# Linear attention with soft mixture of experts on one core: first weight, v, phi and row sums moved

## The chip, the core and the metric

The kernel runs on one core of a Trainium2 chip. The time is device microseconds of that core, the median of three runs. A profile is one execution taken by the hardware profiler; its span is a little shorter than the run's time, since it counts from the first instruction to the last.

The engines are named as in the profile: PE is TensorE (matrix products, with PEld for its weight loads), DVE is VectorE, ACT is ScalarE, POOL is GpSimd, SP only issues transfers. Transfers run on 16 DMA engines, fed by queues: q1 takes those issued by SP and ACT, q0 those issued by POOL, q8 brings instructions.

## The reference

Two steps follow each other. First a linear attention with decay over 768 time steps for 4 batches and 8 heads of size 48; then a layer of soft mixture of experts over the 3072 resulting rows of 384 numbers, with 8 experts of 4 slots.

```python
# attention, for each batch and head: state is D x D
for t in range(S):
    cur = outer(u * k[t], v[t])
    y[t] = r[t] @ (state + cur)
    state = w[:, None] * state + outer(k[t], v[t])

# mixture: x is (N, Dm) = (3072, 384), phi is (Dm, 32)
logits = x @ phi
d = exp(logits) / sum over rows          # dispatch
slot_input = d.T @ x                     # 32 x 384, 4 rows for each of 8 experts
slot_out[e] = relu(slot_input[e] @ w1[e]) @ w2[e]    # w1[e]: 384 x 1024, w2[e]: 1024 x 384
c = exp(logits) / sum over slots         # combine; its sums are the "row sums"
out = c @ slot_out                       # 3072 x 384, f32
```

All inputs and the output are f32. r, k, v are 4.72 MB each, w1 and w2 12.58 MB each, the output 4.72 MB.

## The kernel before

The attention is computed in chunks of 128 time steps, three chunks and two heads at a time: 32 such steps, the loop over i. For each pair of heads m, k and r are scaled by powers of w (`scale`, by POOL from m = 1 on) into `kr`, turned by PE (`t_pe`), and v is cast to bf16 (`v_cast`, by ACT) and put in order by PE with the selection matrix `Q3`. Batches live in three buffers `raw[0..2]`; batch 3 uses `raw[0]` again once batch 0 is used up, and the second-layer weights later take `raw[1]` and `raw[2]`.

The expert weights are loaded by POOL, which casts them to bf16 on the way: first the eight w1, then the eight w2, the last w2 in three parts. `W_AT` says how many are issued in which step. All r, k, v are issued by SP. A small copy into `guard`, which reads one column of the last r, keeps POOL from issuing the first weight before that r has landed.

Routing (logits, their exponentials, the dispatch sums) is done in the loop as rows become complete. After the loop come the first expert layer, the second (`second`, for four experts at a time), the row sums with their reciprocals, and the output: 24 tiles of 128 rows, whose products with `so` are scaled by DVE and ACT in turn and stored in nine transfers. `busy(n)` issues n matmuls whose result is not used, which keep PE's clock up.

```python
    warm = LexpT[:, 2048:2560]
    late = LexpT[:, 2560:3072].bitcast(f32)
    ident_f = late[:, 0:128]
    phi_f = late[:, 128:128 + nM * ES].rearrange("p (m s) -> p m s", m=nM)
    # ... cut ...
    wu = cst.tile([8, 128], f32, name="wu")
    wu3 = wu[:].rearrange("q (e s) -> q e s", s=64)
    O(dve.memset(wu[:], 1.0))
    O(sp.dma_start(out=w_row, in_=w.rearrange("(o h) d -> o (h d)", o=1)))
    O(act.preload_act_table_set("natural_log_exp_and_others"))
    O(dve.memset(warm, 0.0))
    O(dve.memset(one_f, 1.0))
    zt = cst.tile([128, nQ, 3, P2], f32, name="zt")
    O(dve.memset(zt[:], 0.0))
    # ... cut ...
    def load_kr(which, src, b, h0, h1):
        O(sp.dma_start(out=raw_of(which, b).rearrange("p (h x) -> p h x", h=H)[:, h0:h1, :],
                       in_=src[b, h0:h1].rearrange("h (p j) d -> p h (j d)", j=J)))

    def load_v(b, h0, h1):
        O(sp.dma_start(out=raw_of(2, b).rearrange("p (h x) -> p h x", h=H * G)[:, h0 * G:h1 * G, :],
                       in_=v[b, h0:h1].rearrange("h (g p j) d -> p (h g) (j d)", g=G, j=JV)))

    def load_batch(b, step):
        for h0 in range(0, H, step):
            load_kr(0, k, b, h0, h0 + step)
            load_kr(1, r, b, h0, h0 + step)
            load_v(b, h0, h0 + step)

    load_batch(0, 2)
    load_batch(1, 2)
    O(sp.dma_start(out=phi_f, in_=moe_phi.rearrange("(mo p) s -> p mo s", p=128)))
    load_batch(2, H)

    def load_w(n, y0=0, y1=nF):
        if n < E:
            O(pool.dma_start(out=w1_all[:, n, :, :],
                             in_=moe_w1[n].rearrange("(p mo) f -> p mo f", p=128)))
        else:
            O(pool.dma_start(out=w2_of(n - E)[:, y0:y1, :],
                             in_=moe_w2[n - E].rearrange("(p y) d -> p y d", p=128)[:, y0:y1, :]))

    def keep_warm(n, bank=Yb, data=None):
        data = warm if data is None else data
        for _ in range(n):
            O(pe.matmul(bank[:, 0:512], data[:, 0:128], data[:, 0:512], start=True, stop=True))

    # ... cut ...
    QW = 2 * C + JV - 1 + C
    Q3 = cst.tile([128, QW], bf, name="Q3")
    O(pool.memset(Q3[:], 0.0))
    O(pool.affine_select(out=Q3[:], in_=Q3[:], compare_op=ALU.not_equal, fill=1.0, base=JV - 1,
                         pattern=[[-1, QW]], channel_multiplier=JV))
    O(pool.dma_start(out=wu3[0:4, :, 0:D], in_=w.rearrange("(q e) d -> q e d", e=2)))
    O(pool.dma_start(out=wu3[4:8, :, 0:D], in_=u.rearrange("(q e) d -> q e d", e=2)))
    mask_ut = cst.tile([128, 128], f32, name="mask_ut")
    O(pool.memset(mask_ut[:], 0.0))
    O(pool.affine_select(out=mask_ut[:], in_=mask_ut[:], compare_op=ALU.is_ge, fill=1.0, base=0,
                         pattern=[[-1, 128]], channel_multiplier=1))
    # ... cut ...
    def scale(m, j):
        b, q = divmod(m, nQ)
        kr = kr_t[m % NKR]
        src = raw_of(j, b).rearrange("p (h j d) -> p j h d", h=H, j=J)[:, :, 2 * q:2 * q + 2, :]
        eng = dve if m == 0 else pool
        O(eng.tensor_mul(kr[:, j].rearrange("p j (h s) -> p j h s", s=64)[:, :, :, 0:D], src,
                          W[j][:, q].rearrange("p j (h d) -> p j h d", h=2)))
    # ... cut ...
    pend = []
    W_AT = {14: 2, 15: 1, 16: 1, 18: 1, 19: 1, 20: 1, 22: 1, 23: 1, 25: 1, 26: 5}
    T_AT = {-4: [(tt, 0, 1), (tt, 1, 1), (ex, 0, 1), (tt, 0, 2)], -3: [(ex, 1, 1), (ex, 0, 2)],
            -1: [(tt, 1, 2), (ex, 1, 2)], 0: [(tt, 0, 3), (ex, 0, 3)], 1: [(tt, 1, 3), (ex, 1, 3)]}
    Z_AT = {-3: 0, -1: 1, 1: 2, 2: 3}
    # ... cut ...
            let_ev(n0 - 1, None, dve)
        if 0 <= i < nH:
            y_pe(i)
            y_evac(i)
        if odd and 0 <= mu + 3 < nU:
            scale(mu + 3, 0)
        if not odd and 0 <= mu + 2 < nU:
            scale(mu + 2, 1)
        route(i, 0)
        if 0 <= mu + 2 < nU:
            t_pe(mu + 2, odd)
            route(i, 1)
            t_evac(mu + 2, odd)
            if odd and i < 0:
                b_pe(mu + 2)
                b_evac(mu + 2)
        else:
            route(i, 1)
        if odd == 0 and 0 <= mu + 2 < nU:
            v_cast(mu + 2)
        route(i, 2)
    # ... cut ...
        if i == 2:
            O(pool.memset(ones[:], 1.0))
            for t in Le_t:
                O(pool.memset(t[:], 0.0))
        if i == 3:
            load_batch(B - 1, H)
        if 3 <= i < 3 + nM:
            O(act.copy(phi_s[:, i - 3, :].rearrange("p (j g s) -> p g j s", g=2, s=Spe),
                       phi_f[:, i - 3, :].rearrange("p (g j s) -> p g j s", g=2, s=Spe)))
        if i == 28:
            O(pool.memset(uns, 0.0))
        if i == min(W_AT):
            O(pool.tensor_copy(guard[:], raw_of(1, B - 1)[:, 0:1]))
        for _ in range(W_AT.get(i, 0)):
            load_w(nw)
            nw += 1
    assert nw == 2 * E - 1
    for y0, y1 in ((0, 4), (4, 6), (6, 8)):
        load_w(nw, y0, y1)
    # ... cut ...
    def busy(n):
        keep_warm(n, Ab[:, 1, :], w1_all[:, 0, 0, :])
    # ... cut ...
    rsr = cst.tile([128, nN], f32, name="rsr")

    def row_sums(a, z):
        for i in range(a, z):
            O(pe.matmul(Mb[:, i:i + 1], LexpT[:, i:Nn:nN], ones[:, 0:1],
                        start=(i == a), stop=(i == z - 1), skip_group_check=True))

    def row_recip(a, z):
        O(dve.reciprocal(rsr[:, a:z], Mb[:, a:z]))
    # ... cut ...
    def second(g, experts):
        for y in range(nF):
            for x in range(2):
                for j in experts:
                    O(pe.matmul(SO[x][32 * j:32 * j + 32, :], hT[g][:, y, 32 * j:32 * j + 32],
                                w2_of(g * EG + j)[:, y, x * HD:(x + 1) * HD],
                                start=(g == 0 and y == 0), stop=(g == 1 and y == nF - 1), skip_group_check=True))

    second(0, range(EG))
    busy(1)
    second(1, range(EG - 2))
    row_sums(8, nN)
    row_recip(8, nN)
    busy(3)
    second(1, (EG - 2,))
    busy(1)
    second(1, (EG - 1,))
    so = cst.tile([128, Dm], bf, name="so")
    O(dve.tensor_scalar_mul(so[:, 0:HD], SO[0], csr[:, 0:1]))
    O(act.activation(out=so[:, HD:Dm], in_=SO[1], func=AF.Copy, scale=csr[:, 0:1]))
    # ... cut ...
    out_v = out.rearrange("(p n) m -> p n m", n=nN)
    ob = [T1[:].bitcast(f32), T0[:].bitcast(f32), Ab0, Vb[:], Xb[:], Yb[:]]
    sizes = [1, 1, 2, 2, 2, 4, 4, 4, 4]
    obuf = ([raw[0][:, 16 * Dm:17 * Dm], raw[0][:, 17 * Dm:18 * Dm], Wf[0][:, 0:2 * Dm], Wf[1][:, 0:2 * Dm],
             Wf[0][:, 2 * Dm:4 * Dm]]
            + [raw[0][:, x * 4 * Dm:(x + 1) * 4 * Dm] for x in range(4)])

    def emit(i, bank, dst, x0, x1, eng):
        op = ob[bank % 6][:, 0:x1 - x0]
        O(pe.matmul(op, LexpT[:, i:Nn:nN], so[:, x0:x1], start=True, stop=True))
        if eng is dve:
            O(dve.tensor_scalar_mul(dst[:, x0:x1], op, rsr[:, i:i + 1]))
        else:
            O(act.activation(out=dst[:, x0:x1], in_=op, func=AF.Copy, scale=rsr[:, i:i + 1]))

    i = 0
    for gi, sz in enumerate(sizes):
        o_s = obuf[gi][:, 0:sz * Dm].rearrange("p (n m) -> p n m", m=Dm)
        i0 = i
        for j in range(sz):
            if i < 2:
                emit(i, 2 * i, o_s[:, j, :], 0, HD, dve)
                emit(i, 2 * i + 1, o_s[:, j, :], HD, Dm, act)
            else:
                emit(i, i + 2, o_s[:, j, :], 0, Dm, (dve, act)[i % 2])
            i += 1
        O((sp, pool)[gi % 2 if gi > 1 else 0].dma_start(out=out_v[:, i0:i, :], in_=o_s))
```

Of the kernel before, what the change touches and what calls it, by code (L numbers as in the profile page):

```python
# [9 lines left out]
def kernel(  # L10
# [13 lines left out]
    B, H, S, D = r.shape  # L24
    C = 128
    nC = S // C
    Nn, Dm = out.shape
    ES = moe_phi.shape[1]
    E = moe_w1.shape[0]
    F = moe_w1.shape[2]  # L30
    Spe = ES // E
    nM = Dm // C
# [6 lines left out]
    nN = Nn // C  # L39
# [4 lines left out]
    JV = T // C  # L44

    f32 = mybir.dt.float32
    bf = mybir.dt.bfloat16
# [4 lines left out]
    def O(ins):  # L52
        return tc.keep_in_program_order(ins)

    pe, dve, act, pool, sp = nc.tensor, nc.vector, nc.scalar, nc.gpsimd, nc.sync

    big = ctx.enter_context(tc.tile_pool(name="big", bufs=1))
    cst = ctx.enter_context(tc.tile_pool(name="cst", bufs=1))
# [6 lines left out]
    EG = E // 2  # L65
# [8 lines left out]
    def raw_of(which, b):  # L74
        return raw[b % NR][:, which * RW:(which + 1) * RW]
# [6 lines left out]
    Xb = psb.tile([128, 512], f32, name="Xb")  # L82
# [15 lines left out]
    warm = LexpT[:, 2048:2560]  # L98
    late = LexpT[:, 2560:3072].bitcast(f32)
    ident_f = late[:, 0:128]  # L100
    phi_f = late[:, 128:128 + nM * ES].rearrange("p (m s) -> p m s", m=nM)
    wu = cst.tile([8, 128], f32, name="wu")
    wu3 = wu[:].rearrange("q (e s) -> q e s", s=64)
    O(dve.memset(wu[:], 1.0))
    O(sp.dma_start(out=w_row, in_=w.rearrange("(o h) d -> o (h d)", o=1)))
    O(act.preload_act_table_set("natural_log_exp_and_others"))
    O(dve.memset(warm, 0.0))
    O(dve.memset(one_f, 1.0))
    zt = cst.tile([128, nQ, 3, P2], f32, name="zt")
# [2 lines left out]
# [13 lines that stand above are left out]

    load_batch(0, 2)
    load_batch(1, 2)
    O(sp.dma_start(out=phi_f, in_=moe_phi.rearrange("(mo p) s -> p mo s", p=128)))
    load_batch(2, H)

    def load_w(n, y0=0, y1=nF):
# [7 lines left out]
# [3 lines that stand above are left out]
# [9 lines left out]
    Q3 = cst.tile([128, QW], bf, name="Q3")  # L151
    O(pool.memset(Q3[:], 0.0))
    O(pool.affine_select(out=Q3[:], in_=Q3[:], compare_op=ALU.not_equal, fill=1.0, base=JV - 1,
                         pattern=[[-1, QW]], channel_multiplier=JV))
    O(pool.dma_start(out=wu3[0:4, :, 0:D], in_=w.rearrange("(q e) d -> q e d", e=2)))
    O(pool.dma_start(out=wu3[4:8, :, 0:D], in_=u.rearrange("(q e) d -> q e d", e=2)))
    mask_ut = cst.tile([128, 128], f32, name="mask_ut")
    O(pool.memset(mask_ut[:], 0.0))
    O(pool.affine_select(out=mask_ut[:], in_=mask_ut[:], compare_op=ALU.is_ge, fill=1.0, base=0,
# [53 lines left out]
    ones = cst.tile([128, 128], bf, name="ones")  # L213
    Le_t = [cst.tile([128, L, 128], bf, name=f"Le{j}") for j in range(2)]
    phi_s = cst.tile([128, nM, ES], bf, name="phi_s")
    acc = cst.tile([128, NA], f32, name="acc")
    guard = cst.tile([128, 1], f32, name="guard")
    st = {}
# [71 lines left out]
    def a_pe(i):  # L290
        m, b, q, g, n = at(i)
        kT, rT = st["kT", m], st["rT", m]
        for c in range(L):
            t = slice((g * L + c) * C, (g * L + c + 1) * C)
            for e in range(2):
                s = slice(64 * e, 64 * e + 64)
                O(pe.matmul(Ab[:, e, c * C:(c + 1) * C], kT[s, t], rT[s, t]))  # L297
# [129 lines left out]
    def disp_ev(n, ds_p):  # L427
        if n == 0:
            O(dve.tensor_copy(acc[:], ds_p))
        else:  # L430
            O(dve.tensor_add(acc[:], acc[:], ds_p))
# [28 lines left out]
            xt_ev(*ch[s])  # L460

    pend = []
    W_AT = {14: 2, 15: 1, 16: 1, 18: 1, 19: 1, 20: 1, 22: 1, 23: 1, 25: 1, 26: 5}
    T_AT = {-4: [(tt, 0, 1), (tt, 1, 1), (ex, 0, 1), (tt, 0, 2)], -3: [(ex, 1, 1), (ex, 0, 2)],
            -1: [(tt, 1, 2), (ex, 1, 2)], 0: [(tt, 0, 3), (ex, 0, 3)], 1: [(tt, 1, 3), (ex, 1, 3)]}
    Z_AT = {-3: 0, -1: 1, 1: 2, 2: 3}
# [25 lines left out]
    for i in range(-5, nH):  # L492
        mu, odd = divmod(i, 2)
        if 0 <= i + 1 < nH:
            a_pe(i + 1)
            mask_f(i + 1)
        if pend:
            disp_ev(*pend.pop())
        if i == nH - 1:
            turn(n0, (2,), Vb[:].bitcast(bf), act)  # L500
            disp(n0 - 1, ds_t)
            le_t(n0 - 1)
# [4 lines that stand above are left out]
        if 0 <= i + 2 < nH:  # L507
            v_pe(i + 2)
            v_evac(i + 2)
        if 0 <= i + 1 < nH:  # L510
            m_pe(i + 1)
            z_evac(i + 1)
        if odd == 0 and 0 <= mu + 1 < nU:
            prod_f(mu + 1)
        if odd and i > 0 and mu + 2 < nU:
# [19 lines that stand above are left out]
        if i == nH - 3:  # L535
            turn(n0, (0, 1), T0, act)
        if i == nH - 2:
            turn(n1, (0, 1), T1, act)
        for f, j, q in T_AT.get(i, ()):
            f(j, q)  # L540
        if i in (-4, -3):
            wu_steps(i + 4)
        if i in Z_AT:
            q = Z_AT[i]
            O(act.activation(out=zt[:, q, 2, :], in_=zt[:, q, 0, :], func=AF.Copy, scale=wT[:, q:q + 1]))
        if i == 2:
            O(pool.memset(ones[:], 1.0))
            for t in Le_t:
                O(pool.memset(t[:], 0.0))
        if i == 3:  # L550
            load_batch(B - 1, H)
        if 3 <= i < 3 + nM:
            O(act.copy(phi_s[:, i - 3, :].rearrange("p (j g s) -> p g j s", g=2, s=Spe),
                       phi_f[:, i - 3, :].rearrange("p (g j s) -> p g j s", g=2, s=Spe)))
        if i == 28:
            O(pool.memset(uns, 0.0))
        if i == min(W_AT):
            O(pool.tensor_copy(guard[:], raw_of(1, B - 1)[:, 0:1]))
        for _ in range(W_AT.get(i, 0)):
            load_w(nw)  # L560
            nw += 1
# [9 lines left out]
    def busy(n):  # L571
        keep_warm(n, Ab[:, 1, :], w1_all[:, 0, 0, :])
# [33 lines left out]
    for g in range(2):  # L606
        for a in range(2):
            for mi in range(nM):
                for j in range(EG):
                    O(pe.matmul(hb[g][a][32 * j:32 * j + 32, 0:FH], uns[:, mi, g, j, :],  # L610
                                w1_all[:, g * EG + j, mi, a * FH:(a + 1) * FH],
                                start=(mi == 0), stop=(mi == nM - 1), skip_group_check=True))
# [9 lines left out]
# [7 lines that stand above are left out]
# [14 lines left out]
# [6 lines that stand above are left out]
                                start=(g == 0 and y == 0), stop=(g == 1 and y == nF - 1), skip_group_check=True))  # L649

    second(0, range(EG))
    busy(1)
    second(1, range(EG - 2))
    row_sums(8, nN)
    row_recip(8, nN)
    busy(3)
    second(1, (EG - 2,))
    busy(1)
    second(1, (EG - 1,))
    so = cst.tile([128, Dm], bf, name="so")  # L660
    O(dve.tensor_scalar_mul(so[:, 0:HD], SO[0], csr[:, 0:1]))
    O(act.activation(out=so[:, HD:Dm], in_=SO[1], func=AF.Copy, scale=csr[:, 0:1]))

    out_v = out.rearrange("(p n) m -> p n m", n=nN)
    ob = [T1[:].bitcast(f32), T0[:].bitcast(f32), Ab0, Vb[:], Xb[:], Yb[:]]
# [13 lines left out]
# [8 lines that stand above are left out]
            else:  # L687
                emit(i, i + 2, o_s[:, j, :], 0, Dm, (dve, act)[i % 2])
            i += 1
        O((sp, pool)[gi % 2 if gi > 1 else 0].dma_start(out=out_v[:, i0:i, :], in_=o_s))  # L690


# [28 lines left out]
```

The softmax here doesn't subtract the row's maximum and nothing guards it: scores larger than these inputs give would overflow.

## Time and profile before

| what | value |
|---|---|
| median of three runs | 123.75 us (123.72 to 124.0) |
| span of the profile | 122.5 us |
| PE busy | 104.6 us, 85% |
| DVE busy | 96.1 us, 78% |
| ACT busy | 83.5 us, 68% |
| POOL busy | 60.2 us, 49% |
| HBM read, written | 39.38 MB, 4.72 MB |
| scaling by POOL (`kr<-raw,W`) | 30 times, mean 1422 ns |
| row sums on PE (`Mb<-ones,LexpT`) | 24 times, between 95.7 and 101.1 us |
| phi's transfer | one, 48 KB, 5.4 us to landing |
| loads of w and u for `wu` by POOL | one each, 1.5 KB, 4.1 and 4.5 us to landing |
| weight transfers of 768 KB, w1 and w2 | median 13.6 and 19.2 us from issue to landing |

Several engines are busy for most of the span, but their sums do not tell which of them sets the end. A busy share is an average over stages; to find the bound one asks at the end of the span what was waited for last, and follows that back. The sizes of the weight transfers are those in SBUF, as bf16; twice as much is read. The time from issue to landing of a weight is mostly time in the queue behind earlier weights.

### The profile page before, as it was taken

To read this page: it belongs to the slowest core of one execution; us is meant where nothing else is said; L and a number is where in the kernel's file an instruction comes from. 1 tells how busy PE (TensorE), PEld (TensorE's weight loads), DVE (VectorE), ACT (ScalarE), POOL (GpSimd) and SP (SyncE) were. 2 spreads that over 40 slices of the span, in tenths; PEclk is the share of its full clock that TensorE was granted. 3 is DMA by queue.
4 is the path that set the end of the run, shared out by engine and by line. 5 is a ranking of instruction groups with operands and counts; after the bars stand their busy time and mean duration, and the time that the engine had idled before them with its cause. 6 is when DMAs were issued, how large, how long until landed. Compare 5 with 4: busy or idle time off the path is not lost.

```text
span 122.5 us, 4314 instructions
## 1 busy us (share of the span) xinstructions
PE 104.6 (85%) x1790; PEld 83.2 (68%) x1792; DVE 96.1 (78%) x185; ACT 83.5 (68%) x184; POOL 60.2 (49%) x72
## 2 busy tenths in 40 slices
PE   5996797799999999999999999999979997796000
PEld 1465586687788988898888888888855885663000
DVE  6799999999999999899999899999834500299000
ACT  4459668798969998888898888898844500299000
POOL 7729534599999998895877591101000000012000
PEclk9999779999999999999999999999999999999955
DMA  2999999999999999999999999999999998069992
GB/s 57 301 367 367 375 371 370 312 389 364 308 376 382 314 161 210 209 223 214 211 218 217 212 215 215 213 221 211 220 215 212 217 207 159 10 243 381 403 415 98
DMA packets 21173, 31.79 MB, mean 260 GB/s; under 512 B 1377, under 2 KB 18274, under 8 KB 21154
## 3 DMA queue, kind: packets, MB, share of 16 engines
q0 software_dynamic: 3024, 14.55, 54.8%
q1 hardware_dynamic: 18130, 16.96, 41.1%
q8 instruction: 14, 0.23, 0.7%
q14 instruction: 5, 0.04, 0.1%
HBM read 39.38 MB, written 4.72 MB: 360 GB/s over the span
## 4 chain that ended last, share of the span: by engine, by line
PE 43%; DMA 18%; DVE 18%; ACT 7%; issue 4%; POOL 1%; POOLq 0%; DVEq 0%; ACTq 0%
DMA raw<-in_moe_w_dram 18%; PE T L233 7%; PE Vb L282 6%; PE Ab L297 4%; PE Yb L350 4%; DVE prod L255 4%; PE T L245 3%; PE Yb L142 3%; DVE AT L302 3%; PE Mb L323 3%; DVE raw L675 2%; PE Xb L385 2%; PE Yb L363 2%; PE Xb L378 2%; ACT rT L239 2%
## 5 line engine op out<-in xcount | busy, mean ns | idle before, releaser
L226 POOL TENSOR_TENSOR kr<-raw,W 128x576 bf16<-128x576 f32 x30 | 42.2, 1422 | 13.7 <-PE T L233 5.4
L302 DVE TENSOR_TENSOR AT<-Ab,mask_ut 128x768 bf16<-128x768 f32 x32 | 30.3, 946 | 0.8 <-PE Ab L297 0.6
L282 PE MATMUL Vb<-v_bf,Q 128*128 128x96 bf16 x288 | 18.2, 211 | 0.0
L233 PE MATMUL T<-ident,kr 128*128 128x128 bf16 x192 | 16.9, 227 | 1.0 <-POOL kr L226 1.0
L282 PEld LDWEIGHTS <-Q 128*128 128x128 bf16 x288 | 16.4, 101 | 1.5
L239 ACT COPY kT<-T 128x768 bf16<-128x768 bf16 x16 | 12.8, 801 | 4.5 <-PE T L233 3.3
L239 ACT COPY rT<-T 128x768 bf16<-128x768 bf16 x16 | 12.8, 801 | 4.5 <-PE T L233 3.8
L255 DVE TENSOR_TENSOR prod<-T,kT 128x768 bf16<-128x768 bf16 x16 | 15.2, 948 | 0.0
L340 DVE TENSOR_TENSOR dv<-vn,Mb 128x288 bf16<-128x288 bf16 x32 | 14.1, 441 | 0.0
L233 PEld LDWEIGHTS <-kr 128*128 128x128 bf16 x192 | 12.5, 101 | 1.8 <-POOL kr L226 1.2
L288 ACT CAST vn<-Vb 128x288 bf16<-128x288 f32 x32 | 13.4, 419 | 0.1
L339 DVE TENSOR_TENSOR Z<-Mb,zt 128x288 bf16<-128x288 f32 (+1 forms) x32 | 12.7, 397 | 0.8
L370 ACT CAST x<-Yb 128x288 bf16<-128x288 f32 x32 | 13.1, 410 | 0.2
L690 POOL DMA_DIRECT2D out_dram<-W x1 | 0.5, 549 | 25.5 <-DVE W L675 25.5
L297 PE MATMUL Ab<-rT,kT 64*128 64x128 bf16 x192 | 11.1, 222 | 1.5 <-DVE AT L302 1.4
L323 PE MATMUL Mb<-vn,kn 128*128 128x96 bf16 (+2 forms) x80 | 11.3, 239 | 0.0
L350 PE MATMUL Yb<-vn,AT 128*128 128x48 bf16 x192 | 10.4, 186 | 0.1
L268 ACT CAST v_bf<-raw 128x576 bf16<-128x576 f32 x15 | 10.2, 678 | 0.0
L136 POOL DMA_DIRECT2D raw<-in_moe_w_dram x10 | 5.5, 552 | 8.7 <-ACT Le L400 3.5
L363 PE MATMUL Yb<-dv,ident 128*128 128x288 bf16 x32 | 9.3, 289 | 0.2
L350 PEld LDWEIGHTS <-AT 128*128 128x128 bf16 x192 | 7.1, 97 | 3.4 <-issue 0.2
L297 PEld LDWEIGHTS <-kT 64*128 64x128 bf16 x192 | 5.6, 95 | 5.1 <-DVE AT L302 1.4
(142 smaller groups left out, 223.2 us busy)
## 6 DMA issues: line engine op xcount, KB each, us to landing
w_all<-in_moe_w_dram POOLq DMA_DIRECT2D x8, 768.0 KB, 13.6
raw<-in_moe_w_dram POOLq DMA_DIRECT2D x7, 768.0 KB, 19.2
raw<-in_k_dram SPq DMA_DIRECT2D x8, 288.0 KB, 6.2
raw<-in_r_dram SPq DMA_DIRECT2D x8, 288.0 KB, 6.0
raw<-in_v_dram SPq DMA_DIRECT2D x8, 288.0 KB, 6.1
raw<-in_k_dram SPq DMA_DIRECT2D x2, 1152.0 KB, 10.5
raw<-in_r_dram SPq DMA_DIRECT2D x2, 1152.0 KB, 10.1
raw<-in_v_dram SPq DMA_DIRECT2D x2, 1152.0 KB, 11.3
```

What stands on the lines that cost most here:

```text
L226: O(eng.tensor_mul(kr[:, j].rearrange("p j (h s) -> p j h s", s=64)[:, :, :, 0:D], src, W[j][:, q].rearrange("p j (h d) -> p j h d", h=2)))
L233: O(pe.transpose(bank[:, x * C:(x + 1) * C], kr[:, j, x, :], ident[:]))
L239: O(act.copy(t[:].rearrange("p (s j) -> p s j", j=J), bank[:, 0:S].rearrange("p (j s) -> p s j", j=J)))
L255: O(dve.tensor_mul(pr[:].rearrange("p (s j) -> p s j", j=J), T1[:, 0:S].rearrange("p (j s) -> p s j", j=J), st["kT", m][:].rearrange("p (s ...
L282: O(pe.matmul(Vb[:, c * P2:(c + 1) * P2], Q3[:, o:o + C], vb[:, :, g, j, :], start=(j == 0), stop=(j == JV - 1)))
L288: O(act.copy(vn[:].rearrange("p c e d -> p (c e d)"), Vb[:, 0:L * P2]))
L297: O(pe.matmul(Ab[:, e, c * C:(c + 1) * C], kT[s, t], rT[s, t]))
L302: O(dve.tensor_mul(AT[:], Ab[:, :, 0:T].rearrange("p e (c t) -> p e c t", c=L), mask_ut[:, None, None, :].to_broadcast([128, 2, L, C])))
L323: O(pe.matmul(o, kn[:, g * L + c, :], vc, start=first, stop=True, skip_group_check=True))
L340: O(dve.tensor_mul(dv[:], st["v", i][:].rearrange("p c e d -> p (c e) d"), Mb[:, 288:288 + 2 * L, None].to_broadcast([128, L * 2, D])))
L350: O(pe.matmul(Yb[:, o:o + D], AT[:, e, c, :], vn[:, c, e, :], start=first, stop=False, skip_group_check=True))
L370: O(act.copy(st["x", n][:, :, q * P2:(q + 1) * P2], Yb[:, 0:L * P2].rearrange("p (c e) -> p c e", c=L)))
```

## The change

The change has five parts.

- The first weight is issued one step of the loop sooner (step 13, one weight in steps 13 and 14 each in place of two in step 14), and the guard before it reads the last k in place of the last r.
- The last batch's v is loaded in four transfers of two heads each in place of one.
- phi is loaded with three neighbouring rows to a partition, so that each partition gets one piece of 384 B in place of three of 128 B. Then row 3p + j is where row 128 m + p is wanted. PE puts it in order with the selection matrix `Q3`, which did the same for v: nine small matmuls into `Xb`, between a cast by ACT before and a copy by ACT after.
- The two small loads of w and u into `wu` are issued by ACT at the beginning in place of POOL.
- The row sums of tiles 8 to 23 and their reciprocals, and most filler matmuls, are taken out of the wait for the last weights. Tiles 8 to 11 follow the second layer; tiles 12 to 17 and 18 to 23 are done within the output part, when six and twelve tiles have been issued.

What it is for: the weights' transfers begin sooner, small packets are fewer, and PE has nothing else in its order when the last weights land.

```diff
--- before.py
+++ after.py
@@ -98,12 +98,14 @@
     warm = LexpT[:, 2048:2560]
     late = LexpT[:, 2560:3072].bitcast(f32)
     ident_f = late[:, 0:128]
-    phi_f = late[:, 128:128 + nM * ES].rearrange("p (m s) -> p m s", m=nM)
+    phi_f = late[:, 128:128 + nM * ES]
     wu = cst.tile([8, 128], f32, name="wu")
     wu3 = wu[:].rearrange("q (e s) -> q e s", s=64)
     O(dve.memset(wu[:], 1.0))
     O(sp.dma_start(out=w_row, in_=w.rearrange("(o h) d -> o (h d)", o=1)))
     O(act.preload_act_table_set("natural_log_exp_and_others"))
+    O(act.dma_start(out=wu3[0:4, :, 0:D], in_=w.rearrange("(q e) d -> q e d", e=2)))
+    O(act.dma_start(out=wu3[4:8, :, 0:D], in_=u.rearrange("(q e) d -> q e d", e=2)))
     O(dve.memset(warm, 0.0))
     O(dve.memset(one_f, 1.0))
     zt = cst.tile([128, nQ, 3, P2], f32, name="zt")
@@ -125,7 +127,7 @@
 
     load_batch(0, 2)
     load_batch(1, 2)
-    O(sp.dma_start(out=phi_f, in_=moe_phi.rearrange("(mo p) s -> p mo s", p=128)))
+    O(sp.dma_start(out=phi_f, in_=moe_phi.rearrange("(p mo) s -> p (mo s)", mo=nM)))
     load_batch(2, H)
 
     def load_w(n, y0=0, y1=nF):
@@ -152,8 +154,6 @@
     O(pool.memset(Q3[:], 0.0))
     O(pool.affine_select(out=Q3[:], in_=Q3[:], compare_op=ALU.not_equal, fill=1.0, base=JV - 1,
                          pattern=[[-1, QW]], channel_multiplier=JV))
-    O(pool.dma_start(out=wu3[0:4, :, 0:D], in_=w.rearrange("(q e) d -> q e d", e=2)))
-    O(pool.dma_start(out=wu3[4:8, :, 0:D], in_=u.rearrange("(q e) d -> q e d", e=2)))
     mask_ut = cst.tile([128, 128], f32, name="mask_ut")
     O(pool.memset(mask_ut[:], 0.0))
     O(pool.affine_select(out=mask_ut[:], in_=mask_ut[:], compare_op=ALU.is_ge, fill=1.0, base=0,
@@ -213,6 +213,8 @@
     ones = cst.tile([128, 128], bf, name="ones")
     Le_t = [cst.tile([128, L, 128], bf, name=f"Le{j}") for j in range(2)]
     phi_s = cst.tile([128, nM, ES], bf, name="phi_s")
+    phi_b = cst.tile([128, nM * ES], bf, name="phi_b")
+    assert JV == nM
     acc = cst.tile([128, NA], f32, name="acc")
     guard = cst.tile([128, 1], f32, name="guard")
     st = {}
@@ -460,7 +462,7 @@
             xt_ev(*ch[s])
 
     pend = []
-    W_AT = {14: 2, 15: 1, 16: 1, 18: 1, 19: 1, 20: 1, 22: 1, 23: 1, 25: 1, 26: 5}
+    W_AT = {13: 1, 14: 1, 15: 1, 16: 1, 18: 1, 19: 1, 20: 1, 22: 1, 23: 1, 25: 1, 26: 5}
     T_AT = {-4: [(tt, 0, 1), (tt, 1, 1), (ex, 0, 1), (tt, 0, 2)], -3: [(ex, 1, 1), (ex, 0, 2)],
             -1: [(tt, 1, 2), (ex, 1, 2)], 0: [(tt, 0, 3), (ex, 0, 3)], 1: [(tt, 1, 3), (ex, 1, 3)]}
     Z_AT = {-3: 0, -1: 1, 1: 2, 2: 3}
@@ -548,14 +550,25 @@
             for t in Le_t:
                 O(pool.memset(t[:], 0.0))
         if i == 3:
-            load_batch(B - 1, H)
-        if 3 <= i < 3 + nM:
-            O(act.copy(phi_s[:, i - 3, :].rearrange("p (j g s) -> p g j s", g=2, s=Spe),
-                       phi_f[:, i - 3, :].rearrange("p (g j s) -> p g j s", g=2, s=Spe)))
+            load_kr(0, k, B - 1, 0, H)
+            load_kr(1, r, B - 1, 0, H)
+            for h0 in range(0, H, 2):
+                load_v(B - 1, h0, h0 + 2)
+        if i == 5:
+            O(act.copy(phi_b[:], phi_f))
+        if i == 6:
+            for mi in range(nM):
+                for j in range(nM):
+                    o = C * mi - j + nM - 1
+                    O(pe.matmul(Xb[:, mi * ES:(mi + 1) * ES].rearrange("p (j g s) -> p j g s", g=2, s=Spe),
+                                Q3[:, o:o + C],
+                                phi_b[:, j * ES:(j + 1) * ES].rearrange("p (g j s) -> p j g s", g=2, s=Spe),
+                                start=(j == 0), stop=(j == nM - 1)))
+            O(act.copy(phi_s[:].rearrange("p m s -> p (m s)"), Xb[:, 0:nM * ES]))
         if i == 28:
             O(pool.memset(uns, 0.0))
         if i == min(W_AT):
-            O(pool.tensor_copy(guard[:], raw_of(1, B - 1)[:, 0:1]))
+            O(pool.tensor_copy(guard[:], raw_of(0, B - 1)[:, 0:1]))
         for _ in range(W_AT.get(i, 0)):
             load_w(nw)
             nw += 1
@@ -649,17 +662,15 @@
                                 start=(g == 0 and y == 0), stop=(g == 1 and y == nF - 1), skip_group_check=True))
 
     second(0, range(EG))
+    second(1, range(EG - 2))
     busy(1)
-    second(1, range(EG - 2))
-    row_sums(8, nN)
-    row_recip(8, nN)
-    busy(3)
     second(1, (EG - 2,))
-    busy(1)
     second(1, (EG - 1,))
+    row_sums(8, 12)
     so = cst.tile([128, Dm], bf, name="so")
     O(dve.tensor_scalar_mul(so[:, 0:HD], SO[0], csr[:, 0:1]))
     O(act.activation(out=so[:, HD:Dm], in_=SO[1], func=AF.Copy, scale=csr[:, 0:1]))
+    row_recip(8, 12)
 
     out_v = out.rearrange("(p n) m -> p n m", n=nN)
     ob = [T1[:].bitcast(f32), T0[:].bitcast(f32), Ab0, Vb[:], Xb[:], Yb[:]]
@@ -687,6 +698,9 @@
             else:
                 emit(i, i + 2, o_s[:, j, :], 0, Dm, (dve, act)[i % 2])
             i += 1
+            if i in (6, 12):
+                row_sums(i + 6, i + 12)
+                row_recip(i + 6, i + 12)
         O((sp, pool)[gi % 2 if gi > 1 else 0].dma_start(out=out_v[:, i0:i, :], in_=o_s))
```

## The prediction

> **What bounds the kernel now.** I read the page's slices and DMA queues first, then the last part of the chain of waits, then busy time by windows, then GpSimd's timeline where the weights begin.
>
> The page's slices (one digit is a fortieth of the span, tenths of busy; GB/s as written), its queues (packets, MB, share of 16 engines) and its chain by line:
>
> ```profile
> DMA  2999999999999999999999999999999998069992
> GB/s 57 301 367 367 375 371 370 312 389 364 308 376 382 314 161 210 209 223 214 211 218 217 212 215 215 213 221 211 220 215 212 217 207 159 10 243 381 403 415 98
> ...
> q0 software_dynamic: 3024, 14.55, 54.8%
> q1 hardware_dynamic: 18130, 16.96, 41.1%
> q8 instruction: 14, 0.23, 0.7%
> ```
>
> The DMA engines are full in all slices but the first and a hole at slice 35. About 370 GB/s is r, k, v on q1; about 215 is the weights on q0, read as f32 and written as bf16, so twice that is read. GB/s dips at slice 8 and at slices 14 and 15.
>
> The end of the chain of waits (start, us, what):
>
> ```profile
> 83.20 22.45 DMA raw<-in_moe_w_dram
> 105.65 0.04 issue
> 105.69 0.24 PE Xb L647
> ...
> 106.14 0.43 DVE so L661
> 106.56 0.04 issue
> 106.61 0.26 PE T L673
> 106.86 0.03 issue
> 106.89 0.18 DVE raw L675
> ```
>
> The last weight transfer was issued at 83.20 and landed at 105.65, behind all others in one queue. So the weight stream as a whole sets when the output can begin, and what counts is when that stream starts and whether it has holes.
>
> Busy time by windows (span, then busy us and instructions of each engine, granted clock, DMA share, GB/s):
>
> ```profile
> 15.00:21.50 6.50, 5.85 (x97) 4.86 (x97) 6.28 (x12) 4.90 (x11) 2.46 (x2) 0.84 1.10 371
> 21.50:24.50 3.00, 2.13 (x46) 1.85 (x45) 3.00 (x6) 2.15 (x6) 1.59 (x2) 1.00 1.05 311
> 24.50:31.00 6.50, 6.37 (x118) 5.11 (x116) 6.50 (x13) 5.96 (x16) 6.50 (x9) 1.00 1.09 376
> ...
> 41.50:45.50 4.00, 3.94 (x83) 3.32 (x78) 4.00 (x8) 3.76 (x9) 3.96 (x7) 1.00 0.89 184
> 45.50:97.00 51.50, 50.28 (x1023) 42.09 (x1026) 45.07 (x89) 42.03 (x96) 23.83 (x27) 1.00 1.04 215
> ...
> 102.00:106.00 4.00, 3.21 (x33) 2.62 (x32) 0.00 (x0) 0.00 (x0) 0.00 (x0) 1.00 0.46 83
> ```
>
> From 45.5 to 97 the stream runs at a constant 1.04. At 41.5 to 45.5 it is 0.89: the hole between the last v and the first weight. At 102 to 106 it is 0.46: some engines finish well before the last. The packet records of the trace give the detail. Thirteen of the 16 engines end their v at 42.15 to 42.93, three at 43.70 to 43.93; ten get their first weight packet at 43.32 to 43.42, the others up to 44.25.
>
> GpSimd's timeline shows why the first weight is not earlier:
>
> ```profile
> 37.80 4.15 POOL L226 TENSOR_TENSOR kr<-raw,W 128x576 bf16<-128x576 f32 x3
> 41.89 0.20 POOL L558 COPY guard<-raw 128x1 f32<-128x1 f32 x1
> 42.01 1.18 POOL L133 DMA_DIRECT2D w_all<-in_moe_w_dram  x2
> 43.20 1.42 POOL L226 TENSOR_TENSOR kr<-raw,W 128x576 bf16<-128x576 f32 x1
> ```
>
> The guard is not held by the last r: it follows directly on the third of three scalings. The stream starts late because of its place in GpSimd's order. From issue (42.01) to first packet (43.32) is 1.3 us.
>
> **What the Trainium skill says.** (1) "DMA: Bandwidth & Descriptors", section "Issuing engines are not separate DMA queues": transfers of all issuing engines run on the same 16 engines, so another queue saves only the issuer's time. The trace agrees: from 112 to 120 q0 and q1 both store, and together they stay at a share of 0.96 to 1.03. Moving the w and u loads to ACT should thus bring GpSimd's 0.75 + 0.61 us of issue and little more. (2) The same page, "Why a DMA increments its semaphore by 16 and not by 1": the 16 engines finish independently and only the last makes the data usable. Here the last weight's engines land up to 105.65 where the next to last is at 104.64. (3) "Runtime: NRT & Kernel Launch", "Instruction fetch mechanics": instructions arrive in 16 KiB blocks of 256. The page agrees: q8 has 14 packets and 0.23 MB, 14 x 256 = 3584, and TensorE has 1790 + 1792. Each costs one engine 0.7% x 16 x 122.5 / 14 = 0.98 us. (4) "TensorE: Matmul & The Clock Gate", "What's actually happening": the clock is halved after a 3413 ns window without enough work. This trace has it: 0.84 in 15 to 21.5.
>
> **The change part by part.** *First weight sooner.* The guard moves in front of one scaling (1.37 us from start to start in the row of three), from 41.89 to about 40.5; the last k, which it now waits for, has landed by 38.0. Adding 1.3 us from issue, weight packets exist from about 41.9, before the first engine is through with v at 42.15. So each engine passes from v to weights without a gap. The thirteen early engines gain 43.36 - 42.5 = 0.85 us; the three late ones had no gap and gain nothing. The second and third weight keep their times (42.6, 44.5), and successive weights land 3.66 us apart, so nothing runs dry. Expected from this, with the chance that the last engine is one of the three (3/16): 0.85 x 13/16 = 0.7 us.
>
> *phi in longer packets.* 384 packets of 128 B become 128 of 384 B. Window 21.5 to 24.5 moved 311 GB/s against 371 and 376 beside it: 3.0 x (1 - 311/373) = 0.5 us lost. With a third of the packets I take 0.17; of the 0.33 saved 0.25 should arrive at v's end, since q1 has nearly no idle between. The price is on TensorE: nine matmuls with weight loads at i=6, at 0.06 to 0.08 us from start to start as in other small groups, 0.6 us. ACT trades three copies of 0.22 for two of about 0.25. None of this is on the path, for the compute part is done at 99.9 and then waits.
>
> *v in four parts.* The same bytes and packets. It lets the casts wait for their quarter, should the weights slow v's rest. Worth 0, a safety for the first part.
>
> *w and u on ACT.* Their landing (4.1 and 4.5 us after issue) ended at 7.64, and TensorE used them at 7.78 after other work. ACT is idle until 3.9. Worth 0 to 0.1.
>
> *Row sums.* Before, 16 row sums, 1.28 us on TensorE, and four filler matmuls lay between 99.98 and 102 in the wait for weights. If the weights come 1 us sooner these would hold up the second-last expert at 102.55, so they have to go. What they cost later: four row sums after the last expert, 4 x 0.08 = 0.32 us, beside the evacuation of so (106.14 to 106.56), and a reciprocal of 0.2 us on VectorE in its gap from 106.56 to 106.89: 0 to 0.1 us. The two groups of six cost TensorE 0.5 us and VectorE 0.2 each; TensorE is some 0.9 us ahead of VectorE there. The first delays rows 6 and 7, about 0.2 us, at a time when the output queue holds less than 1 us of data; the second is behind 2 us of backlog. I take 0.15 us for the output part.
>
> *Sum.* 0.7 + 0.25 for the weights' landing, and 0.1 because the instruction blocks fall on other engines than in this run, where one fetched at 100.5 made the last engine late: 1.1 us. Less 0.15: 0.95. 123.75 - 0.95 = 122.8 us.
>
> **The rivals.** *A straggler stays.* If the engine that ends last had no gap, its end at 105.65 moves by phi's 0.25 only, and the output part eats half: about 123.6. For it: one engine is 1.0 us later than all others. Against it: the three engines late with v are late by 1.0 to 1.4, which becomes less than the early ones' gain, so the order will mix. *The straggler goes.* The block at 100.5 hits an engine that has been spared; then the next, 104.64, is the last and gains too: 1.0 more, 121.8. TensorE would allow it: second-layer work without row sums and fillers ends at about 103.6. *TensorE becomes the bound.* With fillers gone it idles about 1.3 us before the second-last expert and may lose its clock; output matmuls at half speed would cost up to 0.5 us: 123.3. For it: 0.84 early in the span. Against it: still some 65% busy in that window. *Contention.* Weight packets taking turns with v's small ones stretch v; only the last quarter, needed 20 us later, is touched. Time unchanged.
>
> **Range and chances.** Sure is that 0.6 to 0.9 us of DMA time become usable; open is which engine ends last, 1 us either way, mostly toward less. 8 in 10: 122.0 to 123.6. Faster by over 2% means below 121.28, which needs the lucky straggler and more: 0.06. Slower by over 2% means above 126.2, for which I see no mechanism but a stall of v: 0.02.
>
> **What would show it.** Right: the guard near 40.5, the window 41.5 to 45.5 at a share of 1.0 or more, slice 8 above 340 GB/s, the last weight's landing at 104.0 to 105.0, about 16.8 us from there to the end of the span as now. Wrong: a guard that waits for k, casts of v that wait for DMA around 55, a gap in the output's DMA share at 109 to 112 of over 0.3 us, PEclk of 5 after 100, or a last landing that stays at 105.6.

## The result and the profile after

| kernel | median, us | ratio to before, 95% interval |
|---|---|---|
| before | 123.74 (123.72 to 124.0, four runs) | 1 |
| changed | 122.49 (122.36 to 122.81, four runs) | 0.9898 [0.9874, 0.9922] |

The changed kernel is 1.25 us faster. The two profiled executions are 2.0 us apart in span (122.5 and 120.5): the one of before took 124.25 us, half a microsecond above its median, the one of the changed kernel 122.36. Differences read from the two traces are therefore a little large.

The row of GB/s and the new queue of the changed kernel's page, in the same columns as before:

```profile
GB/s 38 322 362 373 374 367 371 364 391 362 330 380 382 323 204 216 218 213 212 220 206 222 211 220 209 215 215 215 224 208 220 208 206 165 16 261 389 396 420 100
...
q10 hardware_dynamic: 24, 0.00, 0.0%
```

Slice 8 rose from 312 to 364 GB/s, and slices 14 and 15 from 314 and 161 to 323 and 204. q10 is new: ACT's loads of w and u. It is missing in the kernel, below, whose GpSimd issues them again. So what ACT issues has a queue of its own, and q1 holds SP's transfers alone.

GpSimd's timeline at the first weight (start, us, what):

```profile
36.01 4.16 POOL L228 TENSOR_TENSOR kr<-raw,W 128x576 bf16<-128x576 f32 x3
40.09 0.20 POOL L571 COPY guard<-raw 128x1 f32<-128x1 f32 x1
40.22 0.75 POOL L135 DMA_DIRECT2D w_all<-in_moe_w_dram  x1
```

The guard follows the third scaling without a wait, at 40.09 instead of 41.89. Of these 1.80 us, 1.37 are the step of the loop; the rest is GpSimd's whole order lying about 0.4 us earlier. It goes with TensorE's clock: in this execution it was full from 14.26 on, in that of the kernel before it was 0.50 from 13.68 to 17.09 (hence 0.84 from 15 to 21.5).

Busy time by windows (span, then PE, PEld, DVE, ACT, POOL, granted clock, DMA share, GB/s), first of the kernel before:

```profile
42.00:43.00 1.00, 1.00 (x23) 0.98 (x20) 1.00 (x2) 1.00 (x3) 1.00 (x3) 1.00 0.64 189
43.00:44.00 1.00, 0.98 (x20) 0.70 (x19) 1.00 (x3) 0.77 (x3) 0.98 (x2) 1.00 1.06 129
```

The same windows of the changed kernel, and the window that the prediction named:

```profile
42.00:43.00 1.00, 0.98 (x21) 0.78 (x19) 1.00 (x3) 1.00 (x4) 0.98 (x3) 1.00 0.84 181
43.00:44.00 1.00, 1.00 (x26) 0.79 (x22) 1.00 (x3) 0.76 (x3) 1.00 (x1) 1.00 0.98 204
...
41.50:45.50 4.00, 3.94 (x79) 3.40 (x77) 4.00 (x8) 3.75 (x10) 3.96 (x5) 1.00 1.05 212
```

The hole at 41.5 to 45.5 went from a share of 0.89 to 1.05. In windows as short as 1 us, read share and GB/s side by side. From 43 to 44 the kernel before was "busy" at 1.06 and moved 129 GB/s, against 215 for the steady weight stream: the 13 weight packets that began there took 1.09 us each on average, where one of the steady stream takes 0.47. A packet that is on its way counts as busy however slowly its bytes come. Besides, this view books a packet whole in the window where it begins. With each packet spread over its own time, the shares from 42 to 44 are 0.68 and 0.60 in the kernel before, 0.95 and 1.02 in the changed one. And the hole is not gone: from 42 to 43 the changed kernel moved 245 GB/s, weights counted as read, where the steady stream reads 427 (table further below).

The end of the chain of waits:

```profile
81.97 21.82 DMA raw<-in_moe_w_dram
103.79 0.04 issue
...
104.28 0.43 DVE so L671
...
108.39 0.18 DVE rsr L641
```

The last weight landed at 103.79 instead of 105.65, and still ends the wait. From there to the end of the span it is 16.7 us as against 16.85: the row sums that now lie in the output part, whose last reciprocal (`rsr`, 0.18 us at 108.39) shows in the chain, cost nothing that can be seen.

### The profile page after: what moved, and what is told of

It reads as the page before. It is cut to its first block, busy times and chain, and to the rows that moved or that the text cites. A ratio compares the mean times of both kernels' runs of the same rounds, so it can differ in the third digit from the quotient of the medians.

```text
span 120.5 us, 4334 instructions
## 1 busy us (share of the span) xinstructions
PE 102.6 (85%) x1795; PEld 82.9 (69%) x1797; DVE 96.4 (80%) x187; ACT 83.7 (69%) x183; POOL 59.7 (50%) x70
## 4 chain that ended last, share of the span: by engine, by line
PE 37%; DMA 31%; DVE 15%; issue 6%; ACT 1%; POOL 1%; POOLq 0%; DVEq 0%; ACTq 0%
DMA raw<-in_moe_w_dram 31%; PE Vb L284 5%; PE T L235 4%; PE Ab L299 4%; PE Yb L352 3%; DVE W L188 3%; PE T L247 2%; PE Mb L325 2%; DVE prod L257 2%; PE Yb L365 2%; DVE kn L252 2%; DVE Z L341 2%; PE Xb L387 2%; PE Xb L380 2%; PE Yb L144 2%
```

## The experiments

### Which part brings it

*The first weight alone*, in the kernel before:

```diff
-    W_AT = {14: 2, 15: 1, 16: 1, ...}
+    W_AT = {13: 1, 14: 1, 15: 1, 16: 1, ...}
-            O(pool.tensor_copy(guard[:], raw_of(1, B - 1)[:, 0:1]))
+            O(pool.tensor_copy(guard[:], raw_of(0, B - 1)[:, 0:1]))
```

> The kernel before with only the first weight a step sooner (guard on the last k). The theory that the hole in the transfers is the gain: 0.7 us less than before at most, so 123.0, and the 16 row sums and fillers, which now meet the second-last expert's landing, take back up to 0.3, so 123.0 to 123.3. The rival that the gain comes from taking the row sums out of PE's order: no change, 123.7.

Measured: 122.81 us, 0.9911 [0.9897, 0.9925], 1.1 us less than before. This one part brings nearly the whole gain. In its trace the guard is at 40.59, and the window 41.5 to 45.5 has 230 GB/s at a share of 1.08. This execution took 123.27 us, the most of its six. The end of its chain is no longer a transfer (the row sums, the fillers, then the second-last expert):

```profile
100.12 1.21 PE Mb L624 x16
101.34 0.67 PE Ab L142 x3
102.00 0.19 PE Xb L647
...
105.13 0.43 DVE so L661
```

TensorE runs through from the row sums to `so` without waiting, though the last weight packet of this execution began at 103.91. With the weights sooner, the row sums and fillers in their old place became the bound.

*The other four parts without it*: the changed kernel with `W_AT` and the guard as before.

```diff
-    W_AT = {13: 1, 14: 1, 15: 1, 16: 1, ...}
+    W_AT = {14: 2, 15: 1, 16: 1, ...}
-            O(pool.tensor_copy(guard[:], raw_of(0, B - 1)[:, 0:1]))
+            O(pool.tensor_copy(guard[:], raw_of(1, B - 1)[:, 0:1]))
```

> The changed kernel with the first two weights in step 14 again, behind a guard on the last r. If the hole is the gain, 0.7 to 0.9 us more than the changed kernel, 123.2 to 123.4, and the DMA share from 41.5 to 45.5 falls from 1.05 to about 0.9. If the row sums or the start bring the gain, it stays at 122.5.

Measured: 124.14 us, 1.0020 [1.0007, 1.0034]. Without the weight the four other parts make the kernel slightly slower. Within the changed kernel the weight is worth 1.0020 - 0.9898 = 0.0122, or 1.5 us. Its hole is as wide as ever:

```profile
42.00:43.00 1.00, 0.98 (x21) 0.78 (x18) 1.00 (x3) 1.00 (x4) 0.99 (x3) 1.00 0.37 108
43.00:44.00 1.00, 1.00 (x26) 0.79 (x22) 1.00 (x3) 0.76 (x3) 1.00 (x1) 1.00 1.03 103
```

*The row sums alone*, moved in the kernel before:

```diff
     second(0, range(EG))
-    busy(1)
     second(1, range(EG - 2))
-    row_sums(8, nN)
-    row_recip(8, nN)
-    busy(3)
-    second(1, (EG - 2,))
     busy(1)
+    second(1, (EG - 2,))
     second(1, (EG - 1,))
+    row_sums(8, 12)
...
+    row_recip(8, 12)
...
+            if i in (6, 12):
+                row_sums(i + 6, i + 12)
+                row_recip(i + 6, i + 12)
```

> The kernel before with only the row sums and fillers moved. If the weights' landing sets the end, nothing is gained, for nothing else was in the way there: 123.7, or up to 0.15 more for the work in the output part. The rival (PE's order held up the last experts): 0.5 to 1.0 us less, 122.7 to 123.2.

Measured: 124.21 us, 1.0017 [1.0004, 1.0031]. Busy time by windows of this kernel, before and after TensorE's wait of 2.08 us for the second-last expert:

```profile
98.00:101.50 3.50, 1.51 (x31) 1.15 (x26) 0.00 (x0) 0.00 (x0) 0.00 (x0) 1.00 1.05 207
102.00:105.00 3.00, 3.00 (x25) 2.86 (x23) 0.00 (x0) 0.00 (x0) 0.00 (x0) 0.50 0.44 77
```

and the start and end of the two last experts in its chain:

```profile
101.59 0.24 PE Xb L647
...
102.19 0.16 PE Xb L647
102.35 0.16 PE Yb L647
...
105.66 0.43 DVE so L658
```

TensorE idles where the row sums and fillers were, the granted clock falls to 0.50, and the matmuls of the two last experts come every 0.16 us instead of 0.08. They run without a gap to 105.66, although the last weight packet began at 104.77. This is the rival of the lost clock, met here. It agrees with the Trainium skill, "TensorE: Matmul & The Clock Gate", section "HAM oscillation — how this bites in real kernels": a wait for DMA can slow the clock for the work that follows it. But the page warns of idle gaps of over about 3.4 us, and here a gap of 2.08 us came ahead of the slow clock, while the kernel with the late weight, above, waited 2.80 us in the same place and kept 1.00.

The clock's records in the traces account for both. In each trace the clock changes only on a grid of steps of 3.41 us. Here one step ended at 101.84 and held the whole wait: TensorE was busy for 1.33 of its 3.41 us, 39%, and the next step had 0.50. In the kernel with the late weight a step ended at 100.90, in the middle of the wait, and TensorE was busy for 59% of each of the two steps. Over the 14 traces here, from the first record on, each step with TensorE busy for 51% or less was followed by a clock of 0.50, and each with 53% or more by 1.00. So it counts where a wait falls in the grid, and not only how long it is. The grid lies elsewhere in every execution, so one trace tells nothing of the median, and it is not shown that the clock makes up its 0.2 us.

*The row sums back*, in the changed kernel; the reverse of the edit above.

> The changed kernel with row sums and fillers back in the wait for the last weights. The landing of the last weight should not change; PE reaches the second-last expert at about 101.9 in place of 100.6 and needs 2.9 us from there to the end of the second layer, so 104.8 instead of 104.3: 0.3 to 0.6 us more, 122.8 to 123.1. If the fillers' clock matters more than their time, the changed kernel's output part is slower and this one is not slower: 122.5 or less.

Measured: 122.75 us, 0.9901 [0.9888, 0.9914], not to be told from the changed kernel. Its chain shows what the time hides:

```profile
99.62 1.21 PE Mb L637 x16
100.84 0.67 PE Ab L144 x3
...
104.63 0.43 DVE so L674
```

Again TensorE is the bound, and `so` comes at 104.63 instead of 104.28, of which 0.13 us are a later last weight packet (103.64 instead of 103.51). The four kernels form a table of ratios:

| | row sums in the old place | row sums moved |
|---|---|---|
| weight in step 14 | 1 (before) | 1.0017 alone; 1.0020 with v, phi, w and u too |
| weight in step 13 | 0.9911 alone; 0.9901 with v, phi, w and u too | 0.9898 (changed) |

Moving the row sums costs 0.2 us as long as TensorE waits for the weights anyway, and nothing that can be measured when they come sooner.

*phi back* in pieces of 128 B, in the changed kernel:

```diff
-    O(sp.dma_start(out=phi_f, in_=moe_phi.rearrange("(p mo) s -> p (mo s)", mo=nM)))
+    O(sp.dma_start(out=phi_f, in_=moe_phi.rearrange("(mo p) s -> p mo s", p=128)))
...   (and three copies by ACT in place of the nine matmuls)
```

> The changed kernel with phi again in 384 pieces of 128 B, without the nine matmuls. If the small pieces cost DMA time that is not hidden once the hole is closed: 0.25 to 0.4 us more than the changed kernel, so about 0.993 of before (the changed kernel has 0.990). If they cost nothing (the run with only the row sums moved kept v's end at 43.2 with the small pieces): 0.990.

Measured: 122.77 us, 0.9909 [0.9892, 0.9927]. The difference to the changed kernel, 0.0011 or 0.1 us, cannot be told from nothing. Slice 8 has 322 GB/s here, but the kernel with only the row sums moved, also with small pieces, has 358 there: the dip was not phi's alone. The packets themselves are the better measure. The 384 of 128 B took 13 ns each, the 128 of 384 B in the changed kernel 23 ns, so 0.31 and 0.18 us of the 16 engines' time: 0.13 us was all that could be saved.

*w and u by GpSimd again*, in the changed kernel:

```diff
-    O(act.dma_start(out=wu3[0:4, :, 0:D], ...))     # at the beginning; u alike
+    O(pool.dma_start(out=wu3[0:4, :, 0:D], ...))    # where it was; u alike
```

> The changed kernel with the small loads of w and u on POOL again. The prediction gave this part 0 to 0.1: ratio to before 0.990 to 0.991. The rival: POOL's 1.4 us at the start bring the whole row of scalings, and so the guard, 0.4 us forward; then the guard is at 40.5 again in place of 40.1, and the ratio is 0.993.

Measured: 122.68 us, 0.9908 [0.9876, 0.994]. The guard is at 40.08, as in the changed kernel. So the 0.4 us by which the guard is earlier than I had predicted do not come from GpSimd's shorter start.

*The last v in one transfer* again, in the changed kernel:

```diff
-            load_kr(0, k, B - 1, 0, H)
-            load_kr(1, r, B - 1, 0, H)
-            for h0 in range(0, H, 2):
-                load_v(B - 1, h0, h0 + 2)
+            load_batch(B - 1, H)
```

> The changed kernel with the last v in one transfer. The prediction gave this part 0: ratio to before 0.990, and no cast of v that waits for a transfer. If the weights hold up the end of v so far that the first cast of batch 3 (about 55) waits: 0.992 or more.

Measured: 122.56 us, 0.9882 [0.9847, 0.9916]: no difference.

### How much sooner the weight can come

*Step 12*, in the changed kernel, guard included:

```diff
-    W_AT = {13: 1, 14: 1, 15: 1, ...}
+    W_AT = {12: 1, 14: 1, 15: 1, ...}
```

> The changed kernel with the first weight yet a step sooner (step 12, the second in step 14 as now). If only the hole counted, it is closed already and nothing is gained: 0.990. If weight packets that take turns with v also fill what single engines leave idle at v's end (they end v at different times, up to 1 us apart, but each engine can only be full), also 0.990. If v's packets are slow for want of reads in flight and the weights fill them up: up to 0.5 us more, 0.986. If v is held up so that the casts wait: above 0.992.

Measured: 121.73 us, 0.9832 [0.9807, 0.9856]: better than both kernels, 2.1 us below before. Its windows where the changed kernel had shares of 0.84 and 0.98:

```profile
42.00:43.00 1.00, 0.98 (x21) 0.78 (x19) 1.00 (x3) 1.00 (x4) 0.98 (x3) 1.00 1.15 257
43.00:44.00 1.00, 1.00 (x26) 0.79 (x22) 1.00 (x3) 0.76 (x3) 1.00 (x1) 1.00 1.07 221
```

The end of its chain of waits:

```profile
102.86 0.04 issue
...
103.35 0.43 DVE so L671
```

The hole is filled, and the last weight lands 0.93 us sooner than in the changed kernel.

*Step 11, without a guard*:

```diff
-    W_AT = {13: 1, 14: 1, 15: 1, ...}
+    W_AT = {11: 1, 14: 1, 15: 1, ...}
-        if i == min(W_AT):
-            O(pool.tensor_copy(guard[:], raw_of(0, B - 1)[:, 0:1]))
```

> The changed kernel with the first weight in step 11, two steps sooner than now, and without the guard (the first eight weights go to a place of their own). If the gain of step 12 was what was left of the hole, there is no more to be had: 0.983 as there. If weights among the small pieces of v and r make the engines move more in all, the gain goes on by another 0.3 to 0.6 us: 0.978 to 0.981.

Measured: 122.29 us, 0.9851 [0.9814, 0.9887]. With the hole gone at step 12, nothing more is to be had; this interval and that of step 12 overlap. v's last packet comes at 58.68 instead of 43.21; no cast waits for it yet.

*Steps 9 and 12, without a guard*:

```diff
-    W_AT = {13: 1, 14: 1, 15: 1, ...}
+    W_AT = {9: 1, 12: 1, 15: 1, ...}
-        if i == min(W_AT):
-            O(pool.tensor_copy(guard[:], raw_of(0, B - 1)[:, 0:1]))
```

> The same with the first weight in step 9 and the second in step 12. If the hole is all: 0.983 again, as the same work is only put in another order. If the mixing helps: 0.975 to 0.980. If the last k, r and v come too late for their scalings and casts: above 0.985, with POOL waiting for a transfer after 50.

Measured: 131.62 us, 1.0448 [1.0375, 1.0521]. Its executions scatter from 129.05 to 145.33 us, and the interval is that of the lower ones, so take only the sign and the rough size. The DMA engines of this kernel from 45 to 89 us (queue: packets, MB, share):

```profile
q0 software_dynamic: 1599, 8.74, 96.2%
q1 hardware_dynamic: 1392, 0.77, 7.4%
```

and ACT's timeline (in brackets, the wait before it and what ended it):

```profile
89.65 0.67 ACT L269 CAST v_bf<-raw 128x576 bf16<-128x576 f32 x1 [9.63 <-DMA raw<-in_v_dram]
```

The two queues take turns packet by packet, 1392 against 1599. But a full packet of the weights has 6144 B as written, and one of v 576 B: by turns, v gets 0.77 MB through while the weights move 8.74. The Trainium skill says so in "DMA: Bandwidth & Descriptors", section "Queues, rings and completion order": each DMA engine goes round its queues in turn, a packet at a time. By the page a packet can hold several pieces; here 1341 pieces of v went beside 1423 full ones of the weights, about one for one. The last part of v was issued by 45.3 and arrived at 88.9, and the casts waited 9.63 us.

### The start of SP's order

*SP's first load given to ACT*, in the changed kernel, so that SP starts 0.4 us sooner:

```diff
-    O(sp.dma_start(out=w_row, in_=w.rearrange("(o h) d -> o (h d)", o=1)))
+    O(act.dma_start(out=w_row, in_=w.rearrange("(o h) d -> o (h d)", o=1)))
```

> The changed kernel with the load of the row of w issued by ACT, ahead of its table load, so that SP issues the first k at 0.74 instead of 1.14. If the DMA engines are the bound from the first load to the last weight, everything moves 0.4 us forward, and the ratio is 0.987. If the compute part or POOL's order sets the end, it stays at 0.990.

Measured: 122.49 us, 0.9883 [0.9867, 0.9899]. v ends at 42.92 instead of 43.21, but the first weight packet is at 41.66 as before. No clear gain.

*The same with step 12* (both edits):

> The changed kernel with the first weight in step 12 and the row of w issued by ACT, so that SP's loads begin 0.4 us sooner. Alone, the second gave nothing clear (0.988 against 0.990), for v ended 0.3 us sooner but the first weight came no sooner, so the hole grew. With weights waiting behind v already, the 0.3 us should arrive at the end: 0.980 to 0.981. If SP's start is not on the path even then: 0.983 as with step 12 alone.

Measured: 122.29 us, 0.9877 [0.9858, 0.9896]; step 12 alone was better at 0.9832. The two do not add up. SP has a wait from 5.33 to 6.50 in this trace; whether that is the cause was not tried. The hole is filled here too (table below), so a filled hole does not always bring the 0.9832 of step 12.

## Why the prediction came out as it did

The prediction of 122.8 us in a range of 122.0 to 123.6 holds the measured 122.49. The mechanism was the one named: the time of the last weight's landing, set by the hole between v and the weights. The sizes of its terms were not all right.

**The hole, put at 0.85 x 13/16 = 0.7 us: too small.** Alone it was worth 1.1 us, in the changed kernel 1.5. I had measured it by the time in which engines had no packet. What counts is the bytes that did not move. The packet records of the trace, with weight bytes as read (f32) and each packet spread over its own time, give these GB/s for each microsecond. The last column has the start of the packet with which an engine ends its part of the weights, as the mean of the 16 engines and for the latest:

| kernel | 41 to 42 | 42 to 43 | 43 to 44 | 44 to 45 | short of 427 in 42 to 45 | last weight packet |
|---|---|---|---|---|---|---|
| before | 344 | 199 | 125 | 274 | 683 kB = 1.6 us | 103.84, 105.37 |
| weight late, rest changed | 271 | 110 | 112 | 329 | 730 kB = 1.7 us | 103.58, 105.12 |
| weight alone | 328 | 227 | 344 | 430 | 280 kB = 0.7 us | 102.75, 103.91 |
| changed | 275 | 245 | 406 | 431 | 199 kB = 0.5 us | 102.31, 103.51 |
| step 12 | 351 | 417 | 432 | 426 | 6 kB = 0 | 101.62, 102.58 |
| step 12, w row by ACT | 335 | 388 | 428 | 431 | 34 kB = 0.1 us | 101.91, 103.09 |
| step 11 | 405 | 422 | 419 | 405 | 35 kB = 0.1 us | 102.11, 103.36 |

The steady stream has 427; the shortage is the sum of what the three microseconds lack, divided by 427. Between the late weight and the changed kernel it shrinks by 1.2 us; the mean of the last packets moves by 1.3, the latest by 1.6, the median of the time by 1.5. Between the changed kernel and step 12 the four are 0.5, 0.7, 0.9 and 0.8. So the bytes account for most of the gain; the rest lies in how far the latest engine is behind the mean.

The hole of before, 1.6 us, could have been read so from the trace before. It has two parts: engines without a packet, which I had counted, and slow first packets, which I had not. The first sixteen weight packets took 1.02 us each on average in the kernel before, 0.86 in the changed one, 0.51 at step 12 and 0.47 at step 11, which is that of the steady stream. Both parts go when the weights begin while v still fills the engines. Why a first packet is slow otherwise is not shown.

**"So each engine passes from v to weights without a gap": nearly true of the packets, not of the bytes.** The guard came earlier than predicted (40.09, not 40.5), the first packet 1.44 us after the issue (predicted 1.3), and from 42 to 44 the engines had packets for shares of 0.95 and 1.02, where the steady stream has 1.04. Yet 0.5 us of bytes were missing, chiefly since the first packets were slow. Three kernels have this filled, at ratios of 0.9832 (step 12), 0.9851 (step 11) and 0.9877 (step 12 with the row of w), against 0.9898 of the changed kernel. That is 0.3 to 0.8 us, and only the interval of step 12 lies clear of the changed kernel's.

**"The three late ones had no gap and gain nothing", rivals "A straggler stays" and "The straggler goes", 0.1 us for the instruction blocks: not decided.** From before to changed the latest engine's lag behind the mean shrank from 1.5 to 1.2 us. But in the seven kernels of the table it lies anywhere from 1.0 to 1.5 us, with one execution of each, and nothing was run to separate this from chance.

**phi, 0.25 us: too large.** The edit undone changes the time by 0.1, within the uncertainty, and the packets' own times allow 0.13. I had taken the saving from the dip in GB/s. Slice 8 did rise above 340 GB/s as foretold, but in one of the four kernels with the small pieces (358) it does so too, so that sign is weak.

**v in four, 0, and w and u, 0 to 0.1: right.** No cast waited, and each part undone changes nothing measurable.

**The output part, 0.15 us: nothing was seen.** From the landing to the end it takes 16.7 us, before 16.85. (The prediction's sum adds 0.15 here, its list of signs says about 16.8 as before; the two do not agree.)

**"The last weight's landing at 104.0 to 105.0": sooner, 103.79.** The execution traced before was half a microsecond above its median, so of the 1.86 us between the two landings not all is the change.

**"These would hold up the second-last expert ... so they have to go": half right.** With the weights sooner and the row sums back, TensorE does become the bound, and `so` is 0.35 us later in the profile. The time does not show it at step 13. At step 12, where `so` is at 103.35, the old place could cost up to 104.63 - 103.35 = 1.3 us, an estimate from these two traces; that was not run.

**"TensorE becomes the bound" by a lost clock: not in the changed kernel, but in the row sums alone.** There the wait was 2.08 us; in the changed kernel the longest wait for a weight is 0.9 us and the clock stays at 1.00.

**Contention: harmless only within limits.** Time unchanged was right for steps 13 to 11. At step 9 the same taking of turns delays v's end by some 45 us.

So the total of 0.95 against 1.25 is two errors that partly cancel: the weight was worth 1.1 to 1.5 and not 0.7, and the other parts, on which I had counted for 0.2 net, brought nothing that can be told from zero (0.9898 against 0.9911 for the weight alone) or, with the late weight, cost 0.2. The terms as written add up to 0.90, not 0.95. The path was right; that the number came so near is in part luck.

## What to carry to other kernels

Measure a hole between two transfer streams in bytes against the steady rate, not in the busy share of the engines, and start the second stream while the first still fills the engines: here one step sooner than the change did. Not much sooner, because a stream of large packets starves one of small packets that shares its engines. Work moved out of a wait for a transfer gains nothing as long as the transfer comes no sooner; until then it may have been keeping TensorE's clock up. That it pays afterwards shows here only in the traces.

## What was unexpected of the hardware

- The time from a weight's issue to its first packet is no constant: 1.3 us before, 1.44 in the changed kernel, 2.1 at step 12, 3.0 at step 11 and 4.0 at step 9, the longer the more of q1 still lay ahead.
- The first packets of a stream that begins as the other runs out take about twice as long as later ones: 1.02 us against 0.47 in the kernel before, 0.47 at step 11, where v still filled the engines.
- Two queues on the same engines share by packets and not by bytes: in the kernel of step 9, v's 288-KB parts took until 88.9, at 0.77 MB in 44 us.
- TensorE's clock was set anew every 3.41 us by how busy it had been in the step before: 0.50 after 51% or less, 1.00 after 53% or more, in all 14 traces. So a wait of 2.08 us lost the clock and one of 2.80 us, split by the grid, did not.
- The place of GpSimd's order goes with TensorE's clock early on. It became full for the loop at 17.1 us in the trace of the kernel before and at 17.3 with the weight alone, in all others at 15.1 or sooner. In these two the guard is at 41.89 and 40.59; with the guard in the same step but a sooner clock it is at 41.49 (row sums moved) and 40.09 (changed).
